# A delta-rule attention with a multiplicative feed-forward: a new order of all steps on one core

## The chip, the cores and the metric

The kernel runs on one core of a Trainium2 chip. The metric is the time of one execution on the device, in microseconds (us). The profile names the core's engines: PE is the matrix engine (PEld its weight loads), DVE the vector engine, ACT the scalar engine, POOL the general engine, and SP the engine that issues the DMA transfers.

## The reference

```python
# attention: batch 4, heads 8, seq 768, head_dim 48
k_n = k / (norm(k) + 1e-06)
for t in range(S):
    y[:, :, t] = q[:, :, t] @ state
    v_old = k_n[:, :, t] @ state
    state += beta_t * outer(k_n[:, :, t], v[:, :, t] - v_old)
# feed-forward on x = y as (3072 tokens, 384): d_ff 1024
a = x @ w1
b = x @ w2
h = a * b @ w3
out = h @ w_out
```

The weights come as 64-bit floats, q, k, v and beta as 32-bit floats.

## The kernel before

The recurrence over 768 tokens is cut into 12 chunks of 64 tokens (m or c, 0 to 11). Within a chunk the serial updates become a triangular system, which an inverse solves for two chunks at once (j, 0 to 5). The feed-forward takes two chunks of tokens at once as well (u, 0 to 5). w3 and w_out are multiplied into one matrix first, so that the feed-forward is a product with w1 and w2, an elementwise product, and one product with the folded matrix. From u = 1 on these are done by a scheme with seven products instead of eight, with sums of blocks on POOL.

Each part of the work is a Python generator; each `yield` ends a step. A step's name is a part's name, and each time that the name stands in the list ORDER the part runs on to its next `yield`. A prime behind a name moves the copy in that step from ACT to DVE or back. The list is the program order: at the end `in_text_order` ties each instruction to the one before it on its engine, so no scheduler moves anything. Each engine runs its own instructions in the list's order and waits where data, a buffer or a bank of PSUM isn't ready. SP's transfers stand in the same list, so SP can run ahead until a buffer is taken.

The parts, with the lines of their instructions in the profile:

- P0 to P35: the weights. P0 to P7 are w_out (384 KB each), P8 to P23 w3, P24 to P35 w1 and w2 (512 KB each). The first step issues the transfer (L820, through five buffers `raw`), the second converts on ACT (L828, L831), the third shifts on DVE (L833), the fourth adds on POOL (L835).
- k, q, v, beta, p: loads of inputs. k and q are 384 KB a chunk, v 384 KB (two transfers of 192), p loads k and q a second time in another layout (`perm`, `spare`).
- K, Q (L383): transposes of k and q on PE, copied out by L192. From chunk 2 on, d (L369) does it on DVE.
- g and N: squares of k, their sums (L315, L317) and the norms (L324 to L348).
- s (L412, L418 on PE, L424 on DVE, L436 on ACT, L438 on POOL): scores of a chunk.
- u (L475, ACT and POOL): the diagonal blocks, gathered as `columns` for the first two inverses, through DRAM for the others.
- V0 to V5: the inverses, 31 serial steps of two DVE instructions each (L513 and L518 for V0 and V1, L524 and L529 after that). V0 and V1 begin with a transpose of the columns (L495) and end with one back (L532).
- e: the corner of a chunk's inverse. It copies the inverse to its place (L578), transposes it (L588), and multiplies twice on PE (L605).
- c: the chunk's step of the recurrence: three groups of 64 matmuls (L676), each followed by DVE (L707, L716, L736 or L738).
- y (L775 on PE, L796 on ACT): the chunk's output.
- t (L871) and f (L886): transposes of w3 and the fold of w3 and w_out. f is 8 matmuls twice for each of eight row blocks.
- a0, b (L906): the first two chunks' products with w1 and w2. a, h, i, j from 1 on (L1025, L1033): the same in the seven-product scheme. S, G (L1106, L1011): sums of blocks on POOL.
- oA to oD, o5 (L1135) and xA to xD, x5: the last product and its results, with the stores (L1152).

[...]

Of the kernel before, what the change touches and what calls it, by code (L numbers as in the profile page):

```python
# [55 lines left out]
a06 b6 P35 g2 a02 g2 P33 e3 e3 g2 P33 g2 P34 a03 a03 c2 P34 g2 g2 a04 y2 a03 a04 g2 g2 g2 y2 c2 d5
d5 v3 p5 b5 a05 V2 s4 b6 b4 T N2 b5 s4 e3 s4 a05 c2 e3 s4 T s4 s4 d5 k6 e3 n3 n3 s4 a00 e3 d5 s5 s5
b6 s5 s5 s5 s5 g3 T T b7 b7 e3 N2 s5 e3 b4 u4 g3 a00 g3 S0 c3 c3 u5 V2 V2 a07 c3 a07 c3 a06 a06 oD0
g3 V2 oA0 S0 V2 V2 V2 V2 V2 V2 V2 V2 V2 W S0 S0 S0 S0 S0 S0 s4 v4 p6 v5 V2 V2 V2 V2 n5 n5 xA0 y3 y3
oB0 xB0 V2 V2 V2 y3 oA0 S0 S0 S0 S0 G1 d6 S0 S0 S0 S0 c3 oC0 V2 V2 d6 c3 V2 xA0 n4 n4 oB0 xA0 xB0 V2  # L60
W xC0 V2 a10 a10 a10 a10 V2 V2 V2 V2 V2 W j10 k7 oC0 p6 c4 a10 xC0 xC0 xC0 xD0 i10 h10 V2 V2 V2 V2
V2 a10 V2 V2 a12 h10 i10 h10 g3 d6 g3 h10 a12 a12 a12 h10 V2 xD0 e4 j12 a12 d6 a12 h12 i12 e4 i10 g3
e4 p7 h12 g3 i12 W i12 V3 h12 c4 h12 e4 h12 e4 e4 a11 a11 a11 e5 c4 c4 g3 h11 e5 s5 a11 y4 y4 d7 d7
p7 j11 a11 e5 c4 N3 a11 h11 i11 c4 k8 a13 e5 s6 i11 s6 i11 s6 d7 d7 c5 h11 c5 h11 s7 s7 s7 g4 s7 s7
s7 S1 a13 s7 s6 a13 s6 e5 a13 s6 h11 h13 a13 i13 a13 h13 i13 s6 e5 u7 u6 V3 V3 V3 h13 h13 j13 h13
i13 S1 s7 c5 g4 c5 oC1 oA1 g4 g4 V3 V3 V3 V3 V3 V3 V3 V3 V3 V3 V3 y5 S1 S1 oB1 p8 y5 xA1 v6 N3 s6 v7
oD1 oA1 d8 d8 n7 xA1 V3 xB1 V3 V3 V3 V3 V3 V3 S1 S1 y5 oB1 G2 S1 S1 V3 xA1 p8 xB1 V3 c5 n6 c5 xC1
xC1 V3 xD1 xD1 a20 a20 a20 a20 V3 V3 V3 V3 V3 V3 c6 oC1 h20 j20 xC1 a20 V3 V3 V3 a20 V3 h20 i20 a22
n7 n6 h20 V3 V3 h20 c6 i20 k9 g4 xC1 V3 e6 a22 j22 a22 h20 g4 i22 a22 i20 g4 d8 a22 h22 d8 e6 g4 a22
h22 e6 s8 e6 a21 e6 i22 g4 N4 s8 a21 e6 a21 a21 c6 s8 s8 V4 i22 h22 c6 a21 p9 e7 h22 h22 s8 s8 e7 y6  # L70
s8 e7 d9 d9 u8 p9 h21 e7 j21 i21 y6 a21 h21 h21 h21 i21 a23 e7 c6 d9 d9 e7 a23 a23 k10 i21 c6 s9 a23
s9 s9 s9 S2 g5 s9 s9 u9 V4 V4 s9 a23 i23 V4 h21 a23 c7 h23 v9 p10 c7 c7 h23 h23 j23 c7 y7 h23 i23
h23 i23 oD2 S2 oA2 S2 S2 v8 S2 S2 n8 V4 V4 V4 V4 V4 V4 V4 V4 V4 V4 y7 xA2 y7 c7 V4 g5 V4 oA2 xA2 V4
V4 V4 S2 c7 V4 V4 oB2 oC2 xB2 V4 d10 V4 V4 V4 oB2 S2 G3 xA2 xB2 xC2 xD2 V4 V4 d10 k11 xC2 xD2 p10
a30 c8 a30 a30 a30 V4 oC2 xC2 V4 a30 a30 V4 V4 V4 V4 V4 V4 h30 h30 i30 i30 a32 j30 h30 h30 h30 V4 N4
V4 V4 e8 i30 s9 g5 n8 a32 j32 a32 xC2 i32 s8 g5 d10 a32 a32 a32 c8 e8 h32 h32 a31 e8 d10 h32 p11 e8
a31 e8 n9 j31 e8 s10 g5 g5 g5 h32 c8 g5 i32 g5 N5 a31 c8 h32 i32 a31 i31 s10 s10 e9 y8 y8 a31 d11
s10 h31 d11 a31 e9 h31 a33 c8 c8 i31 s10 h31 p11 i31 h31 s10 a33 e9 s10 a33 h33 e9 u10 h31 d11 d11
s11 s11 s11 s11 s11 s11 i33 a33 a33 a33 s11 s11 c9 e9 h33 i33 V5 n9 u11 V5 c9 h33 j33 h33 h33 s10 S3
i33 e9 c9 c9 V5 V5 V5 V5 V5 V5 V5 oA3 y9 oD3 v10 xA3 V5 V5 S3 S3 S3 S3 V5 V5 V5 V5 V5 y9 S3 y9 V5 V5  # L80
V5 oB3 xB3 V5 oA3 S3 S3 V5 V5 V5 V5 c9 oB3 oC3 xB3 G4 n10 xD3 V5 xC3 N5 a40 a40 a40 xC3 xD3 oC3 a40
a40 xA3 j40 V5 V5 xC3 V5 h40 V5 V5 a40 V5 i40 h40 V5 V5 V5 V5 h40 i40 h40 a42 V5 i40 V5 a42 a42 h42
h40 a42 a42 a42 h42 i42 h42 a41 j42 i42 c9 h42 h42 a41 a41 V5 e10 e10 a41 i41 i42 a41 e10 e10 h41
# [2 lines left out]
c11 c11 S4 S4 oB4 xB4 y11 oD4 y11 y11 xC3 S4 S4 oA4 oB4 oC4 xB4 xC4 xC4 S4 S4 a50 oC4 xD4 a50 xD4 G5
xC4 a50 j50 h50 a50 a50 xA4 i50 a50 h50 i50 h50 h50 h50 a52 a52 a52 i52 a52 a52 a52 i50 h52 h52 i52
j52 h52 a51 a51 a51 i52 S5 h52 h51 a51 a51 a51 h51 j51 h52 h51 h51 i51 a53 i51 a53 a53 h53 xA4 xC4
a53 h51 a53 i51 j53 a53 h53 h53 h53 h53 i53 i53 i53 o5 x5 o5 o5 S5 o5 S5 S5 o5 S5 S5 x5 x5 S5 S5 x5
# [1241 lines left out]
```

## Time and profile before

| | |
|---|---|
| time of three executions | 558.93, 560.54, 561.85 us; median 560.54 |
| the profiled execution | 558.04 us |
| its span, first to last instruction | 556.3 us |
| what lies around the span | 1.7 us |
| mean granted clock of PE | 0.988 |
| PE busy | 527.7 us, 95% of the span |
| DVE, POOL, ACT busy | 370.5, 251.1, 182.8 us |

The profile is of one execution. Busy time of PE is taken from the modelled ends of its matmuls. The chain of waits is followed back from the last instruction: each piece is the work, or the wait, that held up the next one. "issue" in it is time in which the engine waited for nothing that the profile shows. A window's row gives the busy time of PE, PEld, DVE, ACT and POOL with the number of instructions, then the granted clock of PE, the mean busy share of the 16 DMA engines, and GB/s. A timeline row gives start and length, the engine and the operation, and in brackets the idle time before it and what ended it.

### The profile page before, as it was taken

Reading aid. Unit: us, or ns where it says so; the run is one execution under the profiler, and the core shown is the slowest. Engines: PE = TensorE matmul, PEld = TensorE weight load, DVE = VectorE, ACT = ScalarE, POOL = GpSimd, SP = SyncE. Lnnn points to the kernel's source line nnn. Section 1 sums busy time; section 2 is a strip of 40 time slices with the busy share of each in tenths; the row PEclk is TensorE's granted clock in tenths of the full one; section 3 lists DMA queues with packets and bytes.
Section 4 is the critical chain, followed back from the end, with each engine's and each line's share of the span. In section 5 each row is a group of like instructions: output and inputs, shape, how many; then the busy total and the mean of one; then the engine's idle time right before and its main releaser. Section 6 shows DMA issues by size and latency. Waiting matters only on the chain.

```text
span 556.3 us, 19847 instructions
## 1 busy us (share of the span) xinstructions
PE 527.7 (95%) x8540; PEld 449.4 (81%) x8540; DVE 370.5 (67%) x826; ACT 182.8 (33%) x384; POOL 251.1 (45%) x275
## 2 busy tenths in 40 slices
...
GB/s 232 259 158 260 174 206 126 152 116 122 81 84 127 93 103 61 67 127 61 121 82 65 94 97 83 92 65 51 88 17 42 73 54 4 7 81 1 0 1 57
DMA packets 197687, 52.64 MB, mean 95 GB/s; under 512 B 185344, under 2 KB 191488, under 8 KB 197600
## 3 DMA queue, kind: packets, MB, share of 16 engines
...
q8 instruction: 67, 1.10, 0.8%
...
## 4 chain that ended last, share of the span: by engine, by line
PE 87%; DVE 4%; DMA 2%; issue 2%; ACT 1%; SPq 1%; POOL 0%; DVEq 0%
PE ps_f L1025 36%; PE ps_f L1135 19%; PE ps_f L906 8%; PE ps_w L676 7%; PE ps_f L886 5%; PE ps_w L775 4%; PE ps_w L605 3%; PE ps_w L412 2%; DMA raw<-in_moe_w_dram 2%; PE ps_w L418 2%; DVE ps_w L518 1%; DVE tb L513 1%; SPq L820 1%; PE ps_w L1135 1%; DVE w L833 1%
## 5 line engine op out<-in xcount | busy, mean ns | idle before, releaser
L1033 DVE TENSOR_TENSOR ab<-ab,ps_f 128x512 f32<-128x512 f32 x80 | 54.4, 682 | 61.6 <-PE ps_f L1025 61.3
L1072 POOL TENSOR_TENSOR ab<-ab,late 128x512 f32<-128x512 f32 x19 | 24.2, 1272 | 131.0 <-DVE ab L1033 131.0
L1025 PE MATMUL ps_f<-xT,w1s 128*128 128x256 f32 x320 | 79.4, 384 | 0.0
L1106 POOL TENSOR_TENSOR ab<-ab 128x512 f32<-128x512 f32 (+1 forms) x56 | 61.2, 1116 | 38.4 <-PE ps_f L1135 28.9
L1025 PEld LDWEIGHTS ps_f<-xT,w1s 128*128 128x128 f32 x320 | 60.6, 192 | 8.3
L1135 PE MATMUL ps_f<-w,ab 128*128 128x192 f32 x376 | 65.5, 328 | 0.0
L1135 PEld LDWEIGHTS ps_f<-w,ab 128*128 128x128 f32 x376 | 61.3, 190 | 1.0 <-issue 0.5
L886 PE MATMUL ps_f<-w2s,w3T 128*128 128x384 f32 x128 | 47.3, 519 | 2.3 <-issue 1.1
L1135 PE MATMUL ps_f<-room,ab 128*128 128x192 f32 x272 | 47.6, 329 | 0.0
L796 ACT COPY xT<-ps_w 48x256 f32<-48x256 f32 x96 | 30.6, 367 | 48.5 <-PE ps_w L775 48.0
L529 DVE TENSOR_TENSOR ps_w<-ps_w,tb 128x31 f32<-128x31 f32 (+15 forms) x124 | 43.3, 349 | 4.3
L1135 PEld LDWEIGHTS ps_f<-room,ab 128*128 128x128 f32 x272 | 44.2, 190 | 0.8 <-issue 0.2
L524 DVE TENSOR_TENSOR tb<-ps_w,Ub 128x31 f32<-128x31 f32 (+15 forms) x124 | 42.0, 339 | 4.3 <-DMA Ub<-Ud 1.1
L438 POOL TENSOR_TENSOR PT<-PT,smask 128x512 f32<-128x512 f32 x20 | 25.5, 1276 | 38.8 <-ACT PT L436 38.8
L1025 PE MATMUL ps_f<-xT,w2s 128*128 128x256 f32 x160 | 41.5, 388 | 0.0
L1025 PE MATMUL ps_f<-xT,room 128*128 128x256 f32 x160 | 41.5, 386 | 0.0
L1041 ACT COPY ab<-ps_f 128x512 f32<-128x512 f32 x20 | 11.7, 586 | 87.1 <-PE ps_f L1025 78.1
L886 PEld LDWEIGHTS ps_f<-w2s,w3T 128*128 128x128 f32 x128 | 24.5, 200 | 19.5 <-issue 3.4
L1025 PE MATMUL ps_f<-x_room,w2s 128*128 128x256 f32 x160 | 39.3, 389 | 0.0
L1025 PEld LDWEIGHTS ps_f<-xT,w2s 128*128 128x128 f32 x160 | 30.6, 194 | 4.3
L1025 PEld LDWEIGHTS ps_f<-x_room,w2s 128*128 128x128 f32 x160 | 29.2, 190 | 5.5 <-DVE late L1033 1.6
L1025 PEld LDWEIGHTS ps_f<-xT,room 128*128 128x128 f32 x160 | 29.4, 190 | 4.9 <-DVE ab L1033 0.6
(145 smaller groups left out, 981.8 us busy)
## 6 DMA issues: line engine op xcount, KB each, us to landing
raw<-in_moe_w_dram SPq DMA_DIRECT2D x16, 512.0 KB, 5.1
ktok<-in_k_dram SPq DMA_DIRECT2D x48, 96.0 KB, 3.4
raw<-in_moe_w_dram SPq DMA_DIRECT2D x24, 192.0 KB, 4.7
vtok<-in_v_dram SPq DMA_DIRECT2D x24, 192.0 KB, 4.4
out_dram<-osb SPq DMA_DIRECT2D x46, 96.0 KB, 1.7
raw<-in_moe_w_out_dram SPq DMA_DIRECT2D x8, 384.0 KB, 4.5
...
```

What stands on the lines that cost most here:

```text
L438: pool.tensor_tensor(out=PT, in0=PT, in1=smask[:].unsqueeze(1).to_broadcast([P, H, C]), op=ALU.mult)
L524: dve.tensor_tensor(out=tv, in0=V[:, 0 : s + 1, s : s + 1].to_broadcast([P, s + 1, n]), in1=U[:, s, s + 1 : BS].unsqueeze(1).to_broadcast( ...
L529: dve.tensor_tensor(out=o, in0=o, in1=tv, op=ALU.subtract)
L676: pe.matmul(out(ps, r, h, z), lhsT=lhs(r, h, z), rhs=rhs(r, h, z), start=True, stop=True,)
L796: act.copy(out=xT[f, p:NP:2, b : b + NR, cc, :].rearrange("p a r t -> p r a t"), in_=pyv[f, z, b : b + NR],)
L886: pe.matmul(ps[:, 0:DM], lhsT=w3Ts[jc, kc // 4][:, kc % 4 * P : kc % 4 * P + P], rhs=wo[:, kc], start=(i == 0), stop=(i == KF - 1),)
L906: pe.matmul(ps[:].rearrange("p b c t -> p b (c t)"), lhsT=w[:, m, js], rhs=x[:, m, :, c0:c1].rearrange("p b c t -> p b (c t)"), start=(m = ...
L1025: pe.matmul(acc[name][:, n * i : n * i + n], lhsT=ws[b][:, P * i : P * i + P], rhs=xs[x], start=new and k == 0 and i == 0, stop=k == len(t ...
L1033: dve.tensor_tensor(out=o_, in0=x, in1=acc[name], op=ALU.add)
L1072: eng.tensor_tensor(out=Z1, in0=Z1, in1=late, op=ALU.mult)
L1106: pool.tensor_tensor(out=o_, in0=x_, in1=y_, op=op)
L1135: pe.matmul(ps[b][:, b, :], lhsT=block(u, HF * f + i, z)[:, P * b : P * b + P], rhs=ws_[w][:, i], start=first and i == 0 and (b == 0 or n ...
```

## The change

The list ORDER is replaced by another one of the same 1470 entries: each part keeps its number of steps and their sequence, and only the place between other parts' steps changes. Some primes change with it, so that some copies out of PSUM go to the other of ACT and DVE. Nothing else in the kernel differs. The first and last lines, and those that hold the steps spoken of below:

```diff
 ORDER = """
-zd P13 P13 P13 zd P13 k0 g0 zp P2 P6 P2 K0 P6 P2 zp P2 k1 K1 P11 P10 g0 g0 K0' K0 K0 P11 P10 g0 g0
-g0 P6 P6 g0 g0 K1' K0 P10 P11 K1' q0 P9 P9 beta zd K1 K1 q1 Q0 P11 V0 P9 P10 Q0' beta g0 Q0 Q0 Q0 s0
-P0 beta N0 P1 P0 P1 P0 s0 Q1 Q1' s0 Q1' P1 P9 zp Q1 Q1 P12 s0 P1 s0 s0 P12 P8 P3 p2 s0 u0 P8 t5 P12
-u0 P12 P0 s1 s1 s1 s1 s1 t2 t4 P3 P5 P8 s1 t4' u1 P8 u1 P3 t5' P3 t3 t2' u1 u0 V0 V0 t1 V0 V0 V0 P5
-s0 t0 t0 P7 t3 t1 P5 P5 V0 V0 V0 d2 P4 P4 P4 k2 P14 P16 P7 P15 V0 V0 V0 P14 P7 P16 P4 g1 g1 f1 f0 g1
...
-t11 f5 f5 V0 V0 V0 V0 e0 e0 d2 e0 P24 d2 t12 P23 e0 e0 e0 N0 P26 t14 P24 s2 v0 P29 e1 P26 N1 s2 s2
...
-t13 u2 e1 P30 c1 c1 t13 s3 s3 s3 s3 s3 s3 u2 f6 y0 P31 c1 c1 P27 u3 u3 u3 V1 V1 V1 P25 P25 V1 V1 V1
-V1 V1 V1 P30 f7 P30 V1 V1 f7 f6 P32 P25 y1 y1 b0 P31 b1 b1 b0 P30 P35 b3 b2 P32 y1 P32 c1 V1 p4 V1
...
-V1 V1 V1 a01 k4 a07 a00 a02 a07 a02 a00 V1 V1 V1 V1 d4 V1 d4 V1 b4 b5 P33 b4 b5 p4 P35 V1 V1 V1 V1
-V1 V1 P34 a01 b1 a02 b6 P35 a01 c1 c2 e2 e2 e2 e2 b1 n2 n2 e2 e2 k5 c2 a06 e2 d4 d4 e2 p5 a03 P34 c2
...
-c10 e10 a41 h41 i41 h41 e11 e11 n10 h41 c10 i41 e10 j41 c10 c10 e11 a43 a43 h43 a43 a43 c10 e11 e11
-e11 h41 a43 a43 h43 i43 i43 c10 h43 xA3 v11 j43 h43 h43 c11 oA4 y10 y10 xA4 n11 i43 S4 S4 n11 c11
...
-o5 x5 x5 o5 x5 x5 x5 x5 x5 x5 x5 x5
+P11 V0 beta P2 P0 P11 P11 P11 P2 beta P3 k0 K0 P0 beta P0 P0 K0' K0 P6 P6 q0 P2 zd P9 P3 Q0 P2 P6 P3
+g0 g0 g0 k1 P8 Q0' P6 P3 g0 Q0' P9 Q0' K0 P9 g0 g0 g0 P9 zp P8 P10 q1 K0' K1 P13 P10 Q0' g0 s0 P12
+P10 P8 g0 zd N0 P10 zp P8 K1' K1 K1' K1 P13 P5 P13 k2 Q1 P1 P13 Q1 Q1 P12 t2 t3 t0 s0 Q1' Q1' P12
+P12 P14 s0 s0 s0 P4 P5 t2 t3' s0 t1 u0 s0 zp u0 t1' s1 s1 s1 t4 t4' t0' P1 u0 P7 P1 s1 s1 s1 P5 P5
+u1 u1 zd t5 u1 f1 p2 v0 P14 P14 P1 V0 V0 V0 V0 g1 V0 g1 V0 P7 P14 P4 V0 P7 V0 P4 P16 s0 P7 P4 zp P15
...
+P20 V0 V0 V0 V1 f4 zp P26 v1 P22 n0 g1 P23 t12 P25 f5 e0 zp e0 e0 f4 g1 e1 f4 d2 d2 e0 e0 zp e0 t14
+e0 e0 p3 d2 e1 P29 s2 n1 t14 t12 N1 zp f5' c0 P26 e1 P23 P21 P25 P29 f7 p3 c0 s2 s2 c0 c0 P26 s2 y0
...
+c1 u2 u2 u2 e1 f6 t15 c1 P25 u3 u3 u3 V1 V1 V1 V1 V1 V1 V1 V1 e1 c1 c1 y0 P25 p4 P32 f6 P24 f7 P27
+f7 P28 y1 y1 V1 V1 P24 V1 V1 P27 V1 P24 b3 b0 b1 b3 b0 P28 V1 V1 V1 V1 d4 c1 c1 g2 P28 y1 P31 P32
+P27 b7 b1 b2 b2 b7 b5 c2 a05 a05 a03 b5 V1 V1 V1 a03 P31 a01 a00 a01 V1 V1 V1 V1 a04 a04 d4 V1 P32
+P30 V1 v2 a00 a06 V1 V1 P30 a06 b6 a02 N1 a02 b6 V1 V1 p4 P31 V1 P30 V1 V1 k5 P32 V2 P31 P35 n2 V1
+V1 a07 P30 b4 b0 e2 g2 n2 e2 e2 e2 e2 a07 e2 c2 P33 a02 e2 d4 d4 b3 b0 g2 g2 g2 g2 g2 g2 p5 e2 b4
...
+V5 V5 xC3 V5 V5 V5 V5 j40 a40 a40 V5 h40 h40 V5 V5 V5 V5 V5 i40 i40 a42 h40 a42 v11 n11 i40 V5 V5 V5
...
+e10 e10 a41 a41 a41 c9 i41 c10 e10 e10 e11 s11 h41 i41 h41 c10 j41 h41 h41 a43 a43 a43 c10 e11 c10
+e11 i43 h43 c10 e11 e11 e11 a43 a43 a43 i41 h43 j43 n11 i43 h43 c10 c11 h43 i43 y10 c11 y10 h43 oD4
...
+S5 S5 xD4 o5 S5 x5 x5 x5 x5 x5 x5 o5 x5 x5 x5 x5
 """
```

More of the change, by code (lines that the diff above doesn't have):

```diff
@@ L45 @@
-P7 f1 zp zp V0 g1 P15 f1 k3 P17 P17 P18 f0 f0 f2 P18 V0 V0 P14 P14 t6 P16 V0 V0 V0 V0 V0 f2 P22 P16
-P19 P15 P17 V0 P18 V0 V0 t6 P22 f2 P15 g1 V0 V0 g1 t7 P19 p2 P20 s1 f3 P18 g1 P17 V0 zp zp zp zp V0
-P19 P22 g1 V0 P19 t7 t8 t8 V0 P24 f3 t10 t9 g1 f4 P22 v1 d2 f3 P20 V0 V0 V0 P20 t9 t10 P20 t11 P24
-t11 f5 f5 V0 V0 V0 V0 e0 e0 d2 e0 P24 d2 t12 P23 e0 e0 e0 N0 P26 t14 P24 s2 v0 P29 e1 P26 N1 s2 s2
-s1 V1 e0 f4 f4' P26 n0 n0 e0 c0 e1 P28 c0 t12' s2 P21 c0 P29 f5' P23 P23 s2 P28 e1 P21 f6 c0 e1 s2
@@ L50 @@
-P29 P28 P26 p3 P21 P23 t15 t15' d3 n1 e1 n1 P29 p3 P25 d3 t14 d3 d3 y0 u2 e1 y0 P28 f7 P21 e1 P32
-t13 u2 e1 P30 c1 c1 t13 s3 s3 s3 s3 s3 s3 u2 f6 y0 P31 c1 c1 P27 u3 u3 u3 V1 V1 V1 P25 P25 V1 V1 V1
-V1 V1 V1 P30 f7 P30 V1 V1 f7 f6 P32 P25 y1 y1 b0 P31 b1 b1 b0 P30 P35 b3 b2 P32 y1 P32 c1 V1 p4 V1
-P31 P31 b0 V1 V1 V1 N1 b2 b3 b2 b3 P27 P27 V1 b0 V1 b2 V1 b3 P27 b7 a01 a05 b7 a04 a04 a05 P33 v2 V1
-V1 V1 V1 a01 k4 a07 a00 a02 a07 a02 a00 V1 V1 V1 V1 d4 V1 d4 V1 b4 b5 P33 b4 b5 p4 P35 V1 V1 V1 V1
@@ L55 @@
-V1 V1 P34 a01 b1 a02 b6 P35 a01 c1 c2 e2 e2 e2 e2 b1 n2 n2 e2 e2 k5 c2 a06 e2 d4 d4 e2 p5 a03 P34 c2
[L56 to L83, printed above, removed]
-c10 e10 a41 h41 i41 h41 e11 e11 n10 h41 c10 i41 e10 j41 c10 c10 e11 a43 a43 h43 a43 a43 c10 e11 e11
@@ L85 @@
-e11 h41 a43 a43 h43 i43 i43 c10 h43 xA3 v11 j43 h43 h43 c11 oA4 y10 y10 xA4 n11 i43 S4 S4 n11 c11
[L86 to L89, printed above, removed]
@@ new lines @@
+P18 V0 V0 V0 V0 V0 V0 V0 g1 s1 t5 k3 f2 f0 P16 t6 P16 N0 P16 zp f0 f0 t6 P15 P17 f2 f1 V0 V0 f1 f2
+P15 P15 s1 t7 t7 f3 f3 P18 P19 P20 P17 V0 d2 V0 g1 V0 g1 P19 P18 V0 P17 P18 V0 V0 P19 P17 n0 t10 f3
+p2 V0 t10 t9 t8 f5 t9 P20 t8 P22 P29 P19 t11 t11 P22 P21 g1 V0 V0 V0 V0 g1 P20 V0 V0 V0 P29 V0 P22
+P20 V0 V0 V0 V1 f4 zp P26 v1 P22 n0 g1 P23 t12 P25 f5 e0 zp e0 e0 f4 g1 e1 f4 d2 d2 e0 e0 zp e0 t14
+e0 e0 p3 d2 e1 P29 s2 n1 t14 t12 N1 zp f5' c0 P26 e1 P23 P21 P25 P29 f7 p3 c0 s2 s2 c0 c0 P26 s2 y0
@@ new lines @@
+y0 P21 k4 s2 d3 e1 P26 s2 P21 d3 f6 t13 P27 P24 P28 n1 e1 t13 e1 d3 d3 s3 P23 P23 s3 s3 s3 s3 s3 t15
+c1 u2 u2 u2 e1 f6 t15 c1 P25 u3 u3 u3 V1 V1 V1 V1 V1 V1 V1 V1 e1 c1 c1 y0 P25 p4 P32 f6 P24 f7 P27
+f7 P28 y1 y1 V1 V1 P24 V1 V1 P27 V1 P24 b3 b0 b1 b3 b0 P28 V1 V1 V1 V1 d4 c1 c1 g2 P28 y1 P31 P32
+P27 b7 b1 b2 b2 b7 b5 c2 a05 a05 a03 b5 V1 V1 V1 a03 P31 a01 a00 a01 V1 V1 V1 V1 a04 a04 d4 V1 P32
+P30 V1 v2 a00 a06 V1 V1 P30 a06 b6 a02 N1 a02 b6 V1 V1 p4 P31 V1 P30 V1 V1 k5 P32 V2 P31 P35 n2 V1
@@ new lines @@
+V1 a07 P30 b4 b0 e2 g2 n2 e2 e2 e2 e2 a07 e2 c2 P33 a02 e2 d4 d4 b3 b0 g2 g2 g2 g2 g2 g2 p5 e2 b4
+P34 c2 P35 P35 b3 c2 a02 a03 g2 a03 e3 y2 v3 N2 a01 a00 b2 c2 P33 P33 d5 d5 P33 e3 y2 s4 P35 P34 P34
+b2 a01 P34 p5 s4 b1 c2 e3 s4 s4 a00 b1 e3 a04 a05 s4 s4 e3 d5 d5 a04 k6 a05 s4 e3 a06 s5 s5 n3 T s5
+s5 T T s5 s5 N2 s5 u4 u5 T b6 b6 n3 a06 V2 a07 a07 e3 c3 b5 b4 b4 b5 b7 b7 oD0 g3 W g3 e3 oA0 c3 V2
+S0 S0 W S0 S0 S0 S0 S0 S0 S0 S0 S0 V2 V2 V2 V2 V2 V2 p6 c3 xA0 S0 s5 s4 V2 V2 c3 V2 oA0 S0 S0 y3 y3
@@ new lines @@
+V2 S0 S0 V2 V2 V2 V2 V2 V2 V2 V2 V2 y3 oB0 xB0 xA0 xA0 G1 V2 oC0 c3 d6 V2 c3 v4 oB0 V2 xB0 V2 xC0 V2
+V2 a10 c4 a10 a10 v5 xC0 oC0 a10 V2 d6 xD0 V2 V2 k7 j10 xC0 p6 a10 V2 V2 h10 V2 V2 i10 a10 h10 n4
+h10 n4 n5 W V2 V2 V2 xC0 c4 h10 xD0 d6 a12 a12 a12 a12 i10 j12 h10 a12 h12 e4 a12 d6 i12 p7 W i10
+h12 e4 e4 h12 e4 e4 e4 a11 e5 g3 i12 i12 h12 g3 g3 g3 a11 a11 c4 a11 h12 c4 v6 e5 g3 g3 g3 i11 y4 y4
+d7 d7 p7 h11 a11 j11 N3 a11 h11 i11 e5 s6 s6 a13 a13 a13 h11 a13 n6 e5 s6 j13 d7 d7 h11 s7 s7 s7 s7
```

22 lines of the change are left out of this document (added).

## The prediction

> **What bounds the kernel now.** I read the page first, its busy times and its chain.
>
> ```profile
> PE 527.7 (95%) x8540; PEld 449.4 (81%) x8540; DVE 370.5 (67%) x826; ACT 182.8 (33%) x384; POOL 251.1 (45%) x275
> PE 87%; DVE 4%; DMA 2%; issue 2%; ACT 1%; SPq 1%; POOL 0%; DVEq 0%
> q8 instruction: 67, 1.10, 0.8%
> ```
>
> TensorE (PE) is busy for 527.7 of 556.3 us and holds 87% of the chain of waits. The change adds no matmul and takes none away, so it can only shift the 28.6 us without one, and the time that matmuls take at a lower clock. The third row is the queue that brings instructions: 1.10 MB in 67 packets is 16.4 KB each. PE has 8540 weight loads, 8540 matmuls and 154 waits and drains in the trace, 17,234 in all, which over 67 is 257: a packet holds 256 PE instructions.
>
> The chain of waits in order of time, around its longest late piece without an engine, and the busy times by window there (PE, weight loads, DVE, ACT, POOL, granted clock, DMA):
>
> ```profile
> 451.30 1.22 PE ps_w L676 x62
> 452.52 0.56 PE ps_w L605 x43
> 453.08 2.54 issue
> 455.88 6.41 PE ps_f L1025 x16
> ```
> ```profile
> 450.90:452.90 2.00, 2.00 (x129) 1.67 (x127) 0.58 (x2) 0.00 (x0) 0.00 (x0) 1.00 0.60 135
> 452.90:455.60 2.70, 0.18 (x21) 0.07 (x9) 0.64 (x1) 0.00 (x0) 0.00 (x0) 0.82 0.49 89
> 455.60:461.50 5.90, 5.88 (x15) 4.69 (x16) 0.00 (x0) 1.63 (x3) 0.83 (x1) 0.51 0.01 3
> ```
>
> PE stands for 2.54 us in "issue": no engine and no transfer of data releases it. After that the granted clock is 0.51 for 5.9 us. What those matmuls should take comes from the rows that price PE's work at full clock:
>
> ```profile
> 496.62 37.64 PE ps_f L1025 x172
> 252.34 10.60 PE ps_f L1135 x64
> 84.31 2.78 PE ps_f L886 x8
> 193.37 1.08 PE ps_w L676 x64
> 208.65 0.69 PE ps_w L605 x50
> 173.07 1.49 PE ps_w L775 x96
> ```
>
> At 37.64/172 = 0.219 us a matmul, 16 matmuls of L1025 need 3.5 us; they took 6.41, so the low clock cost 2.9 us.
>
> **The gap at 453 us.** Counted in order, PE's instruction after the gap is number 15,297 = 59 x 256 + 193. The chain has three more issue pieces of this kind:
>
> ```profile
> 28.16 1.13 issue
> 90.89 0.96 issue
> 95.53 0.81 issue
> ```
>
> They fall at 705, 2241 and 2497, which are 2, 8 and 9 x 256 + 193. So PE stops where a packet ends, and I read the gap as a packet that has not come. Cutting the list into these blocks of 256 and pricing each by the rows above: the block before 15,297 is one step of c10 (64 matmuls of L676) and most of one of e11 (64 of L605), 1.75 us of work. The next packet had that long to arrive, beside this traffic:
>
> ```profile
> q8 instruction: 2, 0.03, 1.4%
> vtok<-in_v_dram SPq DMA_DIRECT2D x2, 192.0 KB, 3.9
> ```
>
> (DMA from 448 to 458 us; a load of 192 KB took 3.9 us to land.) The shortest blocks of the list before, priced so, are 1.75, 2.17, 2.44, 2.52, 2.78, 2.98, 3.01 and 3.04 us. Of the list after they are 3.17, 3.29, 3.36, 3.48 and 3.64. The blocks around steps c10 and e11 are 3.64 and 5.11, and the v11 load, which the list before has some twenty entries behind that step of e11 and SP issued beside it, now stands some sixty ahead of it. The term: -2.5 us for the gap. If a shortened gap stays, it is like the other three rows, 0.8 to 1.1, so -1.4 at the weak end.
>
> The low clock follows the gap, so it goes too: -2.9, and 0 at the weak end, if another pause takes its place. The Trainium skill (TensorE: Matmul & The Clock Gate, "The HAM clock gate") says that the clock halves after an idle window of about 3.4 us whose phase is free-running. The trace shows a pause of 2.54 us followed by 0.51, so here less was enough; by the page's figure alone the term would be 0 and the sum 2.9 us smaller.
>
> The gaps at 90.89 and 95.53 have blocks of 3.23 and 3.34 us; the list after has 3.29 and 3.17 us in the same stretch of heavy loading. Term 0, from -1.8 to +2. The gap at 28.16 lies in the head, which waits for loads anyway.
>
> **The head.** Up to the first fold matmul (L886, step f1) PE has the same steps in both lists, and PE is not the bound there:
>
> ```profile
> 36.64 1.23 PE L871 MATMUL ps_f<-ident,w 128*128 128x128 f32 x8 [2.21 <-DVE w3T L192]
> 38.21 1.25 DVE L495 STREAM_TRANSPOSE Ub<-columns 128x1024 f32<-128x1024 f32 x1 [1.12 <-POOL columns L475]
> 39.33 15.36 PE L886 MATMUL ps_f<-w2s,w3T 128*128 128x384 f32 x38 [0.61 <-POOL w2s L835]
> ```
> ```profile
> 14.00:28.00 14.00, 9.37 (x220) 8.43 (x221) 10.07 (x28) 9.93 (x21) 7.20 (x9) 1.00 0.98 257
> 0.00:38.00 38.00, 21.39 (x485) 18.01 (x486) 21.67 (x47) 25.44 (x44) 22.97 (x33) 1.00 0.82 211
> 28.00:38.00 10.00, 6.38 (x145) 5.20 (x138) 6.98 (x11) 9.03 (x14) 8.90 (x8) 1.00 0.51 116
> 38.00:45.00 7.00, 6.39 (x11) 3.00 (x10) 6.20 (x19) 6.44 (x13) 4.78 (x6) 0.51 1.09 297
> ```
> ```profile
> raw<-in_moe_w_dram SPq DMA_DIRECT2D x16, 512.0 KB, 5.1
> raw<-in_moe_w_out_dram SPq DMA_DIRECT2D x8, 384.0 KB, 4.5
> ktok<-in_k_dram SPq DMA_DIRECT2D x48, 96.0 KB, 3.4
> ```
>
> ACT and POOL are full from 28 to 38 us, and what ends the waits is a copy of w3T, a copy of the columns and a weight piece. I add up what each queue has to do up to f1, with the durations of the same steps in this trace. Ahead of f1 the list before puts 31.5 us on DVE, 35.0 on ACT and 27.2 on POOL; the list after 25.2, 26.6 and 23.1. By 38 us the engines had done 21.7, 25.4 and 23.0 (the row from 0 to 38), so what the list before had beyond that stood ahead in the text only and was no bound. Of transfers, up to the last piece that f1 reads (P5), the list before has 7392 KB (6 of 512, 11 of 384, one of 96), the list after 6624: two of 384 less. Against it, the small loads k0 and q0, which start everything, come behind three weight pieces. And the first DVE step of the inverse V0 (L495) has slightly more ahead of it: DVE 25.7 us for 22.9, ACT 26.6 for 26.0, POOL the same 23.1. So f1 can come earlier, and V0 comes later: at 38.8 us if only ACT's 0.6 counts, at 41.0 if DVE's 2.8 does. I take 41, since DVE has to wait for weight pieces in between.
>
> What that is worth is read at step e0's first product, which needs the end of V0:
>
> ```profile
> 74.61 0.58 PE L605 MATMUL ps_w<-T,U 33*33 33x32 f32 x44
> 69.14 1.25 DVE L532 STREAM_TRANSPOSE Ub<-ps_w 128x1024 f32<-128x1024 f32 x1
> ```
>
> From L495 at 38.21 to L532 at 69.14 are 30.9 us; the list after has 2.1 us less of DVE work among it. So e0's product would come at 74.6 + 2.8 - 2.1 = 75.3. By then PE has done one half fold more (8 matmuls of L886, 2.7 us; f4's second half now stands ahead of e0). Gain 2.7 - 0.7 = 2.0 us, if the folds are ready: they are, f1 starts no later. Range -4 (V0 at 38.8) to +3.
>
> **The second inverse.** Its rows of DVE:
>
> ```profile
> 96.81 0.95 DVE L707 TENSOR_TENSOR vtok<-vtok,ps_w 128x768 f32<-128x768 f32 x1 [2.80 <-PE ps_w L676]
> 102.91 0.96 DVE L716 TENSOR_TENSOR X<-ps_w,wt 128x768 f32<-128x768 f32 x1 [2.58 <-PE ps_w L676]
> 103.78 1.24 DVE L495 STREAM_TRANSPOSE Ub<-columns 128x1024 f32<-128x1024 f32 x1
> 131.23 1.25 DVE L532 STREAM_TRANSPOSE Ub<-ps_w 128x1024 f32<-128x1024 f32 x1
> 134.73 0.71 DVE L588 STREAM_TRANSPOSE T<-TT 128x512 f32<-128x512 f32 x1 [0.75 <-ACT TT L578]
> ```
> ```profile
> 136.33 0.67 PE ps_w L605 x51
> ```
>
> V1's first step stood behind c1's L716, which waited for PE; now it stands right behind L707, so it starts about 5.5 us earlier, at 98.2 (the copies of the columns must come first). Between it and L532 DVE now has 29.7 us instead of 27.45 (two steps of c1 and two weight pieces come in, three products go out). L532 comes at 127.9, L588 3.5 us behind it as now, at 131.4, and e2's first product at about 132.3. That is 4.0 us earlier. But PE has 4.0 us less to do before it (five half products of L906 go behind it, two come ahead, each 1.34), and with the head's gain it would be there at 136.3 - 4.0 - 2.0 = 130.3. It waits 2.0, where the trace has no wait. Term +2.0; from 0, if V1 starts 2 us earlier still, to +4, if it starts that much later.
>
> Everything after that keeps its distances within a few us: each e, c and y step's producers move along with it. Steps whose copies change between ACT and DVE (the primed ones) sum to 0.1 us of DVE. New small waits: 0 to +2, taken as 0. The tail after the last matmul has the same steps in nearly the same order; the last store of xD4 goes down to it, one issue ahead of stores that end later. Term 0.
>
> **The sum**, against the profiled execution (558.04 us, of which 556.30 span): -2.5 - 2.9 + 0 - 2.0 + 2.0 + 0 = -5.4, which is 552.6. That execution was 2.5 us below the median of the runs shown (560.54), where I apply it: 555.1 us.
>
> **Rivals.** *The gap does not hang on the block's length.* PE stands for some other cause, a burst of transfers say (DMA share 0.60 before the gap), and such a pause stays somewhere with its low clock. For it: blocks of 2.17 to 2.52 us show no gap. Against it: all four gaps fall on the same remainder, 193, of 256. Then the first two terms are 0 and the sum is 0: 560.5 us. Chance 0.17. The Trainium skill (Runtime: NRT & Kernel Launch, "Instruction fetch mechanics") speaks for this rival: it says that instructions come in blocks of 256, as the trace shows, but gives PE room for 2048 of them and calls the fetch hidden, so that PE would not stand where one block ends, as it does here four times.
>
> *The gain is paid out again at e2.* At the bound of +4 the wait is longer than the one at 453, so the clock may halve there too: +2.9, and +2.0 for the bound. -5.4 + 2.9 + 2.0 = -0.5: 560.0 us. For it: nothing behind e2 on PE's queue can pass it. Against it: the pauses of 0.96 and 0.81 left the clock at 1.00. Chance 0.08.
>
> *Slower: the head holds V0 back.* Loads of k0 and q0 behind P11, P2, P0 and P3 delay K, the scores, the columns and so V0, whose DVE chain is serial. PE has 33.8 us of work between f1 and e0 and then stands. With V0's first step at T, e0's product moves by T - 38.2 - 2.1 and the term is T - 43.0, plus 2.9 for the clock once PE has stood for 2.5 us. At T = 41 this is the forecast's -2.0; the whole comes to no change at 43.5 (-5.4 + 2.5 + 2.9) and to +2.8 at about 46. At 48: -5.4 + 7.0 + 2.9 = +4.5, 565.0 us. For it: the DMA engines are full (share 0.98 from 14 to 28 us), 1760 KB go ahead of k0 where 512 did, and 4832 KB ahead of q1 where 4064 did, which at 257 GB/s is 3.1 us. Against it: 3.1 us on 38.2 is 41.3, still short of 43.5, and ACT has 0.6 us more ahead of V0 than before and POOL nothing. Chance 0.14.
>
> **How the numbers follow.** Forecast 0.57; the two cases without change 0.25; the slower rival 0.14, and 0.03 for other waits that make it slower; 0.01 for more than the forecast's own bounds. A measurement of this kernel can tell about 0.5% (2.8 us) from no change. Faster 0.58, same 0.25, slower 0.17. The forecast's own range reaches from all the strong ends together, -2.5 - 2.9 - 1.8 - 4.0 + 0 = -11.2 (549.3), to the largest weak end alone, the head at +3 instead of -2, -0.4 (560.1). The range given takes in the cases without change, to 563, which leaves out the 0.17 of the slower ones.
>
> **What would show it.** Right: no issue piece over 1.2 us behind 100 us in the chain, granted clock 1.00 from 60 us to the end, L495's first at 41 us, e0's product at 75, e2's at 132 with a wait of about 2 us, and PE's rows from there to the end taking 6 us less. Wrong: an issue gap at a multiple of 256 plus 193 in a block of over 3 us; a second low-clock stretch; V0 behind 44 us; or waits of PE for DVE or POOL that add up to over 4 us behind 140 us.

## The result, and the profile after

The kernel after took 555.92 us (median of 5 runs, 554.85 to 556.50), the kernel before 561.63 us in its runs up to then (median of 5, 558.93 to 562.82): ratio 0.9904, 95% interval 0.9874 to 0.9934. Two later comparisons, on two chips, gave 0.9887 (0.9848 to 0.9925) and 0.9904 (0.9881 to 0.9928). So the new list is faster by about 1%; 555.1 us with a range of 549.3 to 563.0 had been forecast.

The page of after (profiled execution 555.92 us, span 554.2): PE's busy time, the chain, the instruction queue.

```profile
PE 523.0 (94%) x8540; PEld 447.8 (81%) x8540; DVE 371.1 (67%) x826; ACT 183.1 (33%) x384; POOL 251.2 (45%) x275
PE 79%; DVE 9%; ACT 3%; SPq 2%; issue 2%; DMA 2%; POOL 1%; POOLq 0%; DVEq 0%; ACTq 0%
q8 instruction: 67, 1.10, 0.8%
```

The work is the same: as many matmuls, and 67 instruction packets. PE is busy 4.7 us less for it, in part because fewer of its matmuls ran at the low clock: the granted clock was 0.50 for 11.0 us in this execution and for 13.7 us in that of before. Its time without a matmul grew, from 28.6 to 31.2 us.

The chain of waits of after around steps c10 and e11 (start, length, piece), and two windows there:

```profile
456.33 1.08 PE ps_w L676 x64
457.41 0.72 PE ps_w L605 x52
458.13 3.65 PE ps_f L1025 x16
```
```profile
453.40:457.50 4.10, 4.10 (x109) 3.48 (x109) 1.53 (x4) 0.59 (x1) 0.00 (x0) 1.00 0.27 68
457.50:462.70 5.20, 5.20 (x142) 4.45 (x130) 1.53 (x2) 1.15 (x2) 0.00 (x0) 1.00 0.01 3
```

Where the list before stood for 2.54 us behind L605, the fast matmuls of c10 and e11 now run straight into L1025. The clock is 1.00, and 16 matmuls of L1025 take 3.65 us instead of 6.41. That is what was forecast for this place. Two other issue gaps are in this chain, which the account of the gap below takes up:

```profile
88.59 0.98 issue
325.95 0.46 issue
```

The head and the second inverse went otherwise. DVE's rows of V0, with the row just ahead of it, and of V1, then PE's first product of e0 and of e2:

```profile
41.73 0.83 DVE L833 TENSOR_SCALAR w<-w 128x512 uint32<-128x512 uint32 x1 [2.21 <-ACT w L828]
42.48 1.23 DVE L495 STREAM_TRANSPOSE Ub<-columns 128x1024 f32<-128x1024 f32 x1
72.38 1.25 DVE L532 STREAM_TRANSPOSE Ub<-ps_w 128x1024 f32<-128x1024 f32 x1
99.78 0.95 DVE L707 TENSOR_TENSOR vtok<-vtok,ps_w 128x768 f32<-128x768 f32 x1 [1.29 <-PE ps_w L676]
101.14 1.25 DVE L495 STREAM_TRANSPOSE Ub<-columns 128x1024 f32<-128x1024 f32 x1
131.44 1.25 DVE L532 STREAM_TRANSPOSE Ub<-ps_w 128x1024 f32<-128x1024 f32 x1
```
```profile
76.62 0.56 PE L605 MATMUL ps_w<-T,U 33*33 33x32 f32 x42 [0.64 <-DVE T L588]
135.64 0.76 PE L605 MATMUL ps_w<-T,U 33*33 33x32 f32 x64 [1.15 <-DVE T L588]
```

V0 began at 42.48 (forecast 41) and V1 at 101.14 (98.2); V1's last step, L532, came at 131.44 (127.9) and e2's product at 135.64 (132.3), with a wait of 1.15 us for the inverse (2.0). f1's first product came at 38.76, no later than the 39.33 of before, as forecast. Nor was the clock 1.00 from 60 us on, as forecast: from 76 to 90 us it was 0.88.

To see how much of this is the list and how much one execution, both kernels were traced twice more (before_2, before_3, after_2, after_3). These marks have the same PE work ahead of them in both lists, so their starts (us, first matmul of the step) can be compared:

| first matmul of | before | before_2 | before_3 | after | after_2 | after_3 |
|---|---|---|---|---|---|---|
| c0 (L676) | 80.84 | 80.81 | 81.97 | 81.70 | 81.08 | 81.24 |
| y1 (L775) | 105.55 | 107.57 | 107.44 | 107.40 | 107.64 | 106.99 |
| a10 (L1025) | 187.04 | 190.08 | 189.44 | 189.24 | 189.06 | 189.11 |
| c10 (L676) | 445.94 | 448.56 | 448.49 | 449.19 | 448.53 | 448.27 |
| c11 (L676) | 470.23 | 471.73 | 469.70 | 468.00 | 467.22 | 466.96 |
| o5 (L1135) | 534.12 | 535.61 | 533.58 | 532.00 | 531.22 | 530.97 |
| span | 556.3 | 557.8 | 555.8 | 554.2 | 553.4 | 553.2 |

From c10 to c11 the list before needs 24.29, 23.17 and 21.21 us, the list after 18.81, 18.69 and 18.69: 4.2 us less in the mean. Everywhere else the two lists lie within 1.1 us of each other in the mean, and the trace quoted in the prediction was the earliest of the three at y1 (105.55) by nearly 2 us.

### The profile page after: what moved, and what is told of

It is laid out like the page before. It is cut to its first block, busy times and chain, and to the rows that moved or that the text cites. A ratio compares the mean times of both kernels' runs of the same rounds, so it can differ in the third digit from the quotient of the medians.

```text
span 554.2 us, 19825 instructions
## 1 busy us (share of the span) xinstructions
PE 523.0 (94%) x8540; PEld 447.8 (81%) x8540; DVE 371.1 (67%) x826; ACT 183.1 (33%) x384; POOL 251.2 (45%) x275
## 4 chain that ended last, share of the span: by engine, by line
PE 79%; DVE 9%; ACT 3%; SPq 2%; issue 2%; DMA 2%; POOL 1%; POOLq 0%; DVEq 0%; ACTq 0%
PE ps_f L1025 33%; PE ps_f L1135 20%; PE ps_w L676 5%; PE ps_f L886 5%; PE ps_f L906 5%; PE ps_w L775 4%; PE ps_w L605 2%; PE ps_w L412 2%; DVE ps_w L518 2%; DVE tb L513 2%; PE ps_w L418 1%; ACT columns L475 1%; DMA raw<-in_moe_w_out_dram 1%; DVE w L833 1%; SPq L283 1%
## 5 line engine op out<-in xcount | busy, mean ns | idle before, releaser
L1025 PE MATMUL ps_f<-xT,w1s 128*128 128x256 f32 x320 | 78.1, 381 | 0.0
L1025 PEld LDWEIGHTS ps_f<-xT,w1s 128*128 128x128 f32 x320 | 60.0, 190 | 7.9
L1135 PE MATMUL ps_f<-w,ab 128*128 128x192 f32 x376 | 65.4, 328 | 0.4 <-DVE ab L1062 0.4
L1135 PEld LDWEIGHTS ps_f<-w,ab 128*128 128x128 f32 x376 | 61.4, 190 | 1.5 <-DVE ab L1062 0.5
L1135 PE MATMUL ps_f<-room,ab 128*128 128x192 f32 x272 | 47.6, 329 | 0.0
L886 PE MATMUL ps_f<-w2s,w3T 128*128 128x384 f32 x128 | 45.0, 502 | 0.1
L1135 PEld LDWEIGHTS ps_f<-room,ab 128*128 128x128 f32 x272 | 44.3, 190 | 0.8 <-issue 0.2
L438 POOL TENSOR_TENSOR PT<-PT,smask 128x512 f32<-128x512 f32 x20 | 25.6, 1282 | 37.2 <-ACT PT L436 37.1
L1025 PE MATMUL ps_f<-xT,room 128*128 128x256 f32 x160 | 40.9, 385 | 0.0
L1025 PE MATMUL ps_f<-xT,w2s 128*128 128x256 f32 x160 | 40.4, 383 | 0.0
L1025 PE MATMUL ps_f<-x_room,w2s 128*128 128x256 f32 x160 | 39.2, 388 | 0.0
L1025 PEld LDWEIGHTS ps_f<-x_room,w2s 128*128 128x128 f32 x160 | 29.2, 190 | 5.8 <-DVE late L1033 1.7
L1025 PEld LDWEIGHTS ps_f<-xT,room 128*128 128x128 f32 x160 | 29.5, 190 | 5.1 <-issue 0.6
L1025 PEld LDWEIGHTS ps_f<-xT,w2s 128*128 128x128 f32 x160 | 29.9, 190 | 4.1
```

Of the source, the lines that this page charges most:

```text
L438: pool.tensor_tensor(out=PT, in0=PT, in1=smask[:].unsqueeze(1).to_broadcast([P, H, C]), op=ALU.mult)
L886: pe.matmul(ps[:, 0:DM], lhsT=w3Ts[jc, kc // 4][:, kc % 4 * P : kc % 4 * P + P], rhs=wo[:, kc], start=(i == 0), stop=(i == KF - 1),)
L1025: pe.matmul(acc[name][:, n * i : n * i + n], lhsT=ws[b][:, P * i : P * i + P], rhs=xs[x], start=new and k == 0 and i == 0, stop=k == len(t ...
L1135: pe.matmul(ps[b][:, b, :], lhsT=block(u, HF * f + i, z)[:, P * b : P * b + P], rhs=ws_[w][:, i], start=first and i == 0 and (b == 0 or n ...
```

## The experiments

**The gap and the clock again: before_2, before_3, after_2, after_3.** No edit.

> The kernel before, unchanged, for a second trace. If the gap at instruction 15,297 is made by the short block, it is there again at 2.2 to 2.8 us, whatever else differs between executions. If the half clock behind it belongs to the gap, there is again a stretch of 6.8 us at about half clock right behind it; if the clock's window runs by itself, the stretch may be missing or lie elsewhere, and then the 2.9 us of the prediction's second term belong to single executions and not to the list.

> The kernel before, unchanged, for a third trace; expected as for before_2. The place and number of the half-clock stretches in three traces is what is asked.

> The kernel after, unchanged, for a second trace and for times beside those of the kernel before on this chip. Expected 5 to 6 us under the kernel before again (ratio about 0.990); no gap above 0.5 us at instruction 15,297; V0's first L495 at 42 to 43 us and V1's at 101 as in its first trace; half-clock stretches only ahead of 110 us, behind pauses of PE in the head.

> The kernel after, unchanged, beside the two others on this chip: about 0.989 of the kernel before, no gap above 0.5 us at instruction 15,297; whether half-clock stretches come in the head (none in one of its two traces, two in the other) is what is asked.

The chain of before_2, then of before_3, at the same place, one window of each from the end of the gap on, and the stretch at half clock in the traces of before and before_2:

```profile
455.14 0.56 PE ps_w L605 x43
455.70 2.54 issue
```
```profile
455.06 0.56 PE ps_w L605 x44
455.62 2.26 issue
```
```profile
458.20:464.10 5.90, 5.86 (x45) 4.62 (x47) 0.20 (x1) 1.63 (x3) 0.83 (x1) 0.71 0.01 3
```
```profile
457.90:463.80 5.90, 5.90 (x147) 5.10 (x148) 1.28 (x2) 1.98 (x4) 0.83 (x1) 1.00 0.01 3
```
```profile
454.61:461.44 6.83, 5.83 (x14) 4.67 (x15) 0.00 (x0) 1.63 (x3) 0.83 (x1) 0.50 0.02 4
459.06:462.47 3.41, 3.41 (x10) 2.70 (x9) 0.00 (x0) 1.63 (x3) 0.24 (x1) 0.50 0.02 5
```

The gap stands at instruction 15,297 in each trace, at 2.54, 2.54 and 2.26 us. The clock behind it was 0.51 in the first, 0.71 in the second and 1.00 in the third: half clock for 6.83 us, for 3.41 us, and not at all. So the gap belongs to the list, the low clock behind it to the execution. after_2 (554.59 us, median of 6) and after_3 (554.82, median of 6) have no issue gap there at all. In the stretch from 27 to 47 us the mean clock was 0.83 in all three traces of before, and 0.83, 1.00 and 1.00 in those of after; from 76 to 90 us it was 1.00, 0.76, 0.88 and 0.88, 1.00, 0.88. Over all timed runs the mean granted clock was 0.990 with the list before and 0.997 with the list after.

**Lengthen the short block in the list before: long_block.**

```diff
-c10 c10 e11 a43 a43 h43 a43 a43 c10 e11 e11 e11 h41 a43 a43 h43 i43 i43
+c10 c10 a43 a43 h43 e11 a43 a43 c10 e11 h41 a43 a43 h43 i43 i43 e11 e11
```

> The list before with sixteen entries in a new order around steps c10 and e11, so that the block of 256 PE instructions that ended in the gap at 453 us holds 4.26 us of work instead of 1.75, and the next one 5.11 as before; the v11 load stays where it was. Theory (the gap is the next packet, late behind a short block): no issue gap above 0.5 us between 445 and 470 us, granted clock 1.00 there, and the time is 4 to 6 us under the kernel before (ratio about 0.991). Rival (a pause that comes with the load burst, not with the block): PE still stands for about 2.5 us between 445 and 465 us and the clock halves behind it; the time stays within 1 us of the kernel before.

Chain and a window of long_block:

```profile
451.57 1.23 PE ps_w L676 x64
452.80 2.79 PE ps_f L1025 x12
455.59 0.69 PE ps_w L605 x51
```
```profile
451.20:456.00 4.80, 4.80 (x132) 3.85 (x134) 1.19 (x2) 0.58 (x1) 0.10 (x1) 1.00 0.51 105
```

PE has no idle time at all there, though the load still runs beside it (DMA share 0.51). Twelve matmuls of L1025 now stand between L676 and L605, and the gap is gone: c10 to c11 took 19.25 us. The rival, a pause that comes with the load, falls. The time was 557.20 us against 559.50 for before on the same chip, ratio 0.9956 (0.9933 to 0.9980): 1.1 to 3.7 us less, which holds the 2.3 to 2.5 us of the gap, and not the 4 to 6 expected. Its mean granted clock over the runs was 0.990, nearly that of the list before on this chip (0.991). The traced execution, 553.27 us at a clock of 0.999, was the fastest of its twelve, so its trace doesn't show what the others lost.

**Take the load away and leave the block: v11_early.** The entry `v11` moves from behind `xA3` to 61 entries ahead, behind `a42 a42`.

```diff
-a42 a42 h42
+a42 a42 v11 h42
...
-xA3 v11 j43
+xA3 j43
```

> The list before with the one entry v11 (the load of 192 KB) moved 61 entries up, about where the list after has it; the block ahead of instruction 15,297 stays at 1.75 us of work. Theory (late packet): the gap stays, at 2 us or more, and the time is that of the kernel before within 1 us. Rival (the load burst makes the gap): no gap above 0.5 us there, and the time falls by 3 to 5 us.

The chain of v11_early, and a window of the gap:

```profile
455.59 0.56 PE ps_w L605 x43
456.15 2.01 issue
```
```profile
456.10:458.20 2.10, 0.09 (x6) 0.04 (x1) 0.51 (x1) 0.00 (x0) 0.00 (x0) 1.00 0.00 0
```

The DMA share in the gap is 0.00 instead of 0.49, and the gap is 2.01 us. So the load costs at most 0.2 to 0.5 us of it (the three traces with the load differ by 0.28 themselves), and the rest comes without it. The time was 559.73 us, ratio 0.9986 (0.9956 to 1.0015): no difference that can be told.

**Make the block short again in the list after: after_short and after_short2.**

```diff
# after_short
-j41 h41 h41 a43 a43 a43 c10 e11 c10 e11 i43
+j41 h41 h41 c10 e11 c10 e11 a43 a43 a43 i43
# after_short2
-i41 h41 c10 j41 h41 h41 a43 a43 a43 c10 e11 c10 e11 i43
+i41 h41 c10 a43 a43 c10 e11 c10 e11 j41 h41 h41 a43 i43
```

> The list after with three entries of a43 put behind e11's third, so that the block ahead of instruction 15,297 holds 1.95 us of work instead of 3.64; nothing else moves, and the v11 load stays some sixty entries ahead. Theory (late packet): a gap of 2 to 2.6 us ends that block, near 457 us, and the time rises by 2 us over the kernel after if the clock stays up, by about 5 if it halves behind the gap (558 to 561 us). Rival (the load burst made the gap): no gap above 0.5 us there, 556 us as the kernel after.

> The list after with nine entries around steps c10, e11 and a43 in another order, so that instruction 15,297 falls a few instructions behind c10.3's wait (as in the list before, where it falls at that wait) and the block that it opens holds 2.06 us of work; in after_short, whose block held 1.95 us, it fell on the last matmul ahead of the wait. Theory, refined (the next packet is asked for when PE's sequencer passes the boundary, which a wait in front of it holds up, and comes some 4.5 us later): a gap of 2 to 2.6 us ends the block, and the time rises by 2 to 3 us over the kernel after, more where the clock halves behind it. Rival (after_short had no gap because only the old list's traffic makes one): no gap above 0.6 us, and the time of the kernel after within 1 us.

Pieces of the chain of after_short, then of after_short2, with the window behind the latter's gap:

```profile
457.92 0.71 DVE T L588
458.77 0.72 PE ps_w L605 x46
459.49 0.37 issue
```
```profile
456.35 0.41 PE ps_f L1025
456.77 1.19 issue
457.95 5.99 PE ps_f L1025 x27
```
```profile
458.00:463.90 5.90, 5.90 (x31) 4.92 (x30) 1.37 (x2) 0.00 (x0) 0.00 (x0) 1.00 0.01 3
```

In after_short e11's products had to wait for their operand (T, L588), which stretched the short block while the packet came: 0.37 us of gap was left, 2.0 to 2.6 had been expected. Its time, 557.45 us, ratio to before 0.9955 (0.9928 to 0.9983), is on the chip of long_block, where after was not run, so it decides little. In after_short2 the same place has a gap of 1.19 us in a list that had none, with no load beside it (share 0.01 in the gap). Its time is 556.51 us beside 554.82 of after_3 on the same chip: 1.7 us more. So a short block at this place made a gap in either list; that its size is 4.5 us less the block's work, as expected there, does not hold (2.4 by that, 1.19 measured). Taken from the DMA records, the packet was asked for 0.41 us behind the start of the block in after_short2, and 2.12, 2.15 and 2.00 us behind it in the three traces of before. What sets that moment stays open. What is constant is the end: in all these gaps PE went on 1.2 to 1.6 us after the packet had landed.

**The head: after_kq.** The loads of k and q move up in the list after.

```diff
-P11 V0 beta P2 P0 P11 P11 P11 P2 beta P3 k0 ... P6 P6 q0 ... g0 g0 g0 k1 ... P10 q1
+P11 k0 V0 beta P2 P0 P11 P11 P11 P2 beta P3 q0 ... P6 k1 P6 ... g0 g0 q1 g0 ... P10
```

> The list after with its four first loads of k and q moved up (k0 behind the first load of P11, q0 to where k0 was, k1 to where q0 was, q1 to where k1 was). Theory A (the head was held by these loads, which stood behind weight pieces): V0's first L495 comes at about 39.5 us instead of 42.5, e0's product at about 74 instead of 76.6, V1's first at 99 or earlier instead of 101.1, and the time is 1.5 to 3 us under the kernel after (about 553.5 us). Theory B (the order of the weight pieces on DVE, ACT and POOL holds the head): L495 moves by less than 1 us and the time stays within 1 us of the kernel after.

PE's longest waits up to 50 us in after_kq, then in after_3; then V0's first row in after_kq, and pieces of the two chains to it, after_kq's first:

```profile
PE ps_f L1224 <- DMA beta_fm<-in_beta_dram: 7.9, 1, 7.9
PE ps_f L383 <- DVE KQ L192: 7.1, 1, 7.1
PE ps_f L383 <- ACT KQ L192: 2.3, 1, 2.3
```
```profile
PE ps_f L1224 <- DMA beta_fm<-in_beta_dram: 5.5, 1, 5.5
PE ps_f L383 <- DVE KQ L192: 5.5, 1, 5.5
PE ps_f L383 <- DMA ktok<-in_k_dram: 3.8, 2, 3.3
```
```profile
44.60 1.23 DVE L495 STREAM_TRANSPOSE Ub<-columns 128x1024 f32<-128x1024 f32 x1
```
```profile
19.78 5.80 DMA raw<-in_moe_w_dram
27.61 0.70 DVE seed L324
```
```profile
24.96 0.71 DVE seed L324
```

Neither theory: the waits for k are gone, but beta comes 2.4 us later, the wait for a copy on DVE ends at the same time as in after_3 (22.64 and 22.66 us), one of 2.3 us for a copy on ACT is new, and V0 begins at 44.60, 2.1 to 2.7 us later than in the traces of after. The time was 557.94 us, ratio to before 0.9981 (0.9953 to 1.0008), where after had 0.989 to 0.990 in its three comparisons. The 2.65 us against after_3 are already there where DVE begins the norms of k (L324), at 27.61 instead of 24.96: in after_kq the chain to it goes through the load of a weight piece, landed at 25.6 us, that DVE shifts first. Moving these four loads up doesn't bring V0 forward; which order of loads would is not shown.

**Old head, new rest: hy_bA_y2.** The list before up to the first y2, then the remaining entries in after's order.

```diff
 (before, up to y2)
+(all entries of after that are left, in after's order)
```

> The list before up to the first entry of y2, then all that is left in the order of the list after. By the two traces the new list had lost 3.1 us against the old one at y2 (work of PE ahead counted) and won 5.4 between c10 and c11. Theory: the two parts are independent, so this list keeps the old head and drops the late gap: V0's first L495 at 38.2 us, no issue gap above 1 us behind 140 us, clock 1.00 from 60 us on, and the time 2 to 3.5 us under the kernel after (about 553 us). Rival (the part ahead of y2 makes no difference by itself; a wait later in the list takes it back): within 1 us of the kernel after, 556 us.

PE's longest wait behind 140 us, then a piece of the chain:

```profile
PE ps_f L906 <- DVE ab L922: 5.2, 1, 5.2
```
```profile
409.63 1.76 issue
```

565.07 us, ratio 1.0097 (1.0061 to 1.0133): a loss from the seam. The chain has seven issues of L283 on SP there, one behind another from 153.25 us on, then the transfer to `perm` and DVE's L369, and PE waits for DVE for 5.2 us: the loads of one list's order came too late for the other's. V0 began at 38.5, and from c10 to c11 it needs 18.84 us, as after. But it has an issue gap of 1.76 us at instruction 13,761 (53 x 256 + 193), where none above 1 us was expected, behind a block with 4.7 us of PE work. The question of the head stays unanswered by it.

**The second inverse: after_v1.** In the list after, 33 entries ahead of y1 are reordered (the expectation says 42): s3 stands ahead of two entries of e1, the copies u2 and u3 stand together behind these, and V1's first two entries ahead of c1's second. In it e1's product reads the buffer U after s3 has replaced it (U has two buffers in turn), so that part of the recurrence is not computed with its own values; every instruction still runs.

```diff
-f6 t13 P27 P24 P28 n1 e1 t13 e1 d3 d3 s3 P23 P23 s3 s3 s3 s3 s3 t15 c1 u2 u2 u2 e1 f6 t15 c1 P25 u3 u3 u3 V1 V1 ...
+f6 d3 d3 s3 s3 s3 s3 s3 s3 t13 P27 P24 P28 n1 e1 t13 e1 u2 u2 u2 u3 u3 u3 P23 P23 t15 c1 e1 f6 V1 V1 t15 c1 P25 ...
```

> The list after with 42 entries ahead of y1 in a new order: the steps s3 and its two copies of columns (u2, u3) stand some ten entries earlier, and the second inverse's first two entries ahead of c1's second. Theory (what after lost at e2 is the late start of V1, held by the copies of the columns and by c1's L707): V1's L495 at 99 to 100 us instead of 101.5, e2's product 1 to 2 us earlier, the time 1 to 2 us under the kernel after (553 us). Rival (PE is there as late anyway, held by packets between 83 and 105 us): e2's product within 0.5 us of 135.5, the time within 0.7 us of the kernel after.

Its chain of waits ahead of V1:

```profile
99.11 0.58 ACT late L630
...
99.71 1.08 ACT columns L475
...
103.03 1.11 ACT columns L475
...
104.23 1.25 DVE Ub L495
```

V1 began at 104.23 instead of 100.7 to 101.5, and the time was 559.64 us, 4.8 us more than after_3 on the same chip. The copies of the columns stood behind e1's copies (L630) on ACT's queue, and those behind PE's later e1. Both theories missed: four copies of 1.1 us one behind another on ACT set V1's start here, where DVE stood idle 4.95 us for the last of them.

## Why the prediction was right, and where it was not

**The gap: right as a term, half right as a rule.** Forecast -2.5; the three traces of before have 2.54, 2.54 and 2.26 us, those of after none. long_block removes it by the order within 16 entries, v11_early keeps 2.01 of it without the load, after_short2 makes one of 1.19 in the new list. The rival that the load makes it explains at most 0.2 to 0.5 us. But the work in a block does not decide alone. The prediction's sign of being wrong, an issue gap at a multiple of 256 plus 193 in a block of over 3 us, came up: the traces of after have 0.98 to 1.17 us at instruction 1,985, where PE was busy for 4.3 to 4.5 us in the block, and 0.46 to 0.47 us at 11,201, with 4.3, and hy_bA_y2 has its 1.76 with 4.7. (By the same count the block ahead of 15,297, priced at 1.75, held 2.16.) In these three the packet was asked for late, 2.3 to 3.7 us behind the start of the block. So the time of the request counts as much as the block's work, and what sets it is not shown. The Trainium skill (Runtime: NRT & Kernel Launch, "Instruction fetch mechanics") gives PE room for 2048 instructions and calls the fetch hidden. The runs do not agree: PE stood up to 2.54 us where one block of 256 ended, and went on 1.2 to 1.6 us after the next packet had landed.

**The low clock behind it: mis-sized, as a term of the median.** -2.9 is what the first trace had, with half clock for 6.83 us, but before_2 had it for 3.41, and before_3 and v11_early none behind gaps of 2.26 and 2.01 us. From c10 to c11 the gain was 5.5, 4.5 and 2.5 us, 4.2 in the mean and not 5.4. The step that failed is "The low clock follows the gap, so it goes too": a single execution's stretch was taken for the list's. The Trainium skill (TensorE: Matmul & The Clock Gate, "The HAM clock gate") has the window free-running, so that the cost varies from run to run. The traces agree with that part: the same gap of 2.54 us was followed by 6.83 us of half clock and by 3.41.

**The head: wrong in sign, by 2.5 us in the means.** V0's L495 came at 42.48, 42.34 and 41.95 us in the traces of after where 41.0 was forecast, and the stretch from L495 to L532 was 29.9 us where 28.8 was (30.9 less 2.1). So L532 was 2.6 us late by the forecast, and e0's product came at 76.62 instead of 75.3. The slower rival, which turns on the same step, put the point of no change at V0 = 43.5; 1.0 to 1.6 us were left to it. At y1, with equal work ahead, after stands 0.5 us behind before in the mean of three, where the term said 2.0 ahead. The step that failed is V0 "at 41.0 if DVE's 2.8 does", a sum of the work ahead on DVE. It does not hold the waits within that order: in each trace of after DVE is idle for 2.2 to 2.3 us just ahead of L495, until ACT, behind its copies of the columns, has converted a weight piece (L828), and shifts that piece first (the row at 41.73). The last copy of the columns had ended 1.3 us before L495 began. No run moves this piece, so what V0 would gain without it is not shown.

**The second inverse: mis-sized the other way.** V1's start at 101.14 instead of 98.2 follows from the step that placed it "right behind L707": only a weight piece's shift of 0.42 us stands between the two, but L707 itself came at 99.78 and not at 96.81. That 96.81, which the forecast took over, was the earliest of the three traces of before by 1.9 us (98.84 and 98.71 in the others). The copies of the columns end at the same time, at 101.0. e2 waits 1.15 us for it, where 2.0 was forecast. Yet from y1 to a10, equal work again, after needs 81.8 us and before 82.0 in the mean of three. So the term, +2.0, is 0 as measured at a10: before_2 and before_3 have an issue gap of their own there (0.92 us at 143.98 and 0.64 at 143.54, both at instruction 4,033, behind 3.3 us of PE work), which the list after has not.

**Other gaps.** Forecast 0. Ahead of 100 us both lists keep such gaps: after's chain has 0.98 us at 88.59, before's 0.96 and 0.81; from a10 to c10 after needs 0.7 us more (259.5 to 258.8 in the means), of which the gap at 11,201 is 0.46 to 0.47 in each of its traces; those of before have no gap in that stretch. None of over 1.2 us stands behind 100 us in the traces of after, as forecast.

**The sum.** By equal marks: +0.5 up to y1, -0.2 to a10, +0.7 to c10, -4.2 to c11, +0.1 to the end, -3.0 in the mean span (553.6 against 556.6). The forecast was -5.4, the medians differ by 5.3 to 5.7. The three traced executions of before took 558.04, 559.52 and 557.51 us, under its medians on their chips (561.63 and 560.33), while those of after (555.92, 555.13, 554.88) lie at theirs. So some 2.5 us of the difference in the medians lie in executions that no trace shows. The mean clocks of the runs (0.990 and 0.997) point to more low-clock stretches in the list before, but the traced executions of before have 0.988, 0.985 and 0.991, no more than its runs, and long_block gained 2.3 us at 0.990. The cause of that part stays open. That the forecast's number came within 0.8 us of the result is luck to that extent: the shortfall of the late term and of the head was made up by a difference that the traces do not hold. One sign was also set beside its own sum: PE's rows from e2 on were to take 6 us less, but the forecast's own marks (e2 at 132.3, the end 5.4 us earlier) leave 1.4, since work moves behind e2; the first traces have 420.0 and 418.6 us.
